# An eleventh pattern buffer, a ring of 23, and another order of the work in an attention and feed-forward kernel

## The chip, the cores and the metric

The kernel runs on one core of a Trainium2 chip. The metric is the device time of one execution in microseconds (us). Three timed runs of the kernel before took 674.03 to 674.70 us, with the median at 674.62. The core has five engines: PE (TensorE, matmuls into the eight banks of PSUM), ACT (ScalarE), DVE (VectorE), POOL (GpSimd) and SP (SyncE, which issues the DMAs here). Each works through its own list of instructions in order, and waits on semaphores for the others.

## The reference

The input x has 2048 rows of 640. It is normalised by rows, and three things are added up: x itself, an attention and a feed-forward part that both read the normalised rows.

```python
xn = _layernorm(x, axis=-1)
# attention: 32 heads of 20, one k and one v for all heads
q = (xn @ wq) as [32 heads, 2048, 20];  k = xn @ wk;  v = xn @ wv
p = softmax(q @ k.T * 20 ** -0.5)
A = (p @ v) put together as [2048, 640] @ wo
# feed-forward, 1536 wide, squared ReLU
h = relu(xn @ w1 + b1);  B = (h * h) @ w2 + b2
return x + A + B
```

The softmax's 32 x 2048 x 2048 exponentials are the bulk of the work.

## The kernel before

**Tiles.** Queries come in 4 chunks (`qc`) of 512 rows, heads in 8 groups (`g`) of 4: 32 blocks (`b`). A block has 16 tiles of 128 keys. A tile of a block is four scores matmuls (one per head, side by side on four row groups of PE, L1395), each filling one bank with 128 keys x 512 queries. One bank of such scores is called a head-tile here: there are 32 x 16 x 4 = 2048.

**Two ways to an exponential.** Most tiles go through ACT: one ACTIVATE (L1676, in `S_EXP`) reads two or three neighbouring banks and writes exp into slots of a ring `PT` with `RING` slots of 512 columns. A slot is free again when the PV matmul (L1981, in `PVblk`) has read it. The other tiles go through DVE: it turns a bank of scores into 16-bit integers that are the bits of a bf16 power of two (L1775, in `S_P1`), into a pattern buffer of `pbx`; there are `NPB` buffers of four heads. Three further buffers of the tile get the same pattern plus a constant (phases), by DVE (L1796, in `S_PH`) or by POOL as 64-bit integer additions (L1858, in `S_PHP`). All four patterns are multiplied with v, the three phases with weighted copies `vp`, so that their sum smooths the staircase of the first. `ph_take` (L1751) hands out free pattern buffers.

**PV and norm.** PV matmuls of a block add up in one bank; v has a column of ones, so that the softmax's denominators come along. When a block is done, `norm` (L2005) copies the bank (`Tn`, L2026), sends the denominators through DMAs (`dn`, reciprocal L2031, `kT`'s spare rows, `Rb` spread over the partitions), multiplies (L2042) into `OTs`, and `pack` moves the rows by DMA into `OTp`, where the head rows of a chunk stand closely for the output matmuls. The last three blocks (`norm_last`, L2049) do this with transposes on DVE instead. The last two blocks' rows go to a buffer of their own, `OT7`, and meet rows of `wo` in `wo_u`.

**The other work.** The feed-forward matmuls (L1013), the projections of q, k and v, and the output matmuls are put in between as units with due positions (`U`, `S_MISC`). PE is kept from going idle by filler matmuls (L1896, `S_FILL`).

**What sets the order.** The whole order is worked out while the program is built. `Sched` (L262) runs the streams (`S_QK`, `S_EXP`, `S_P1`, ...) against a model of the engines' durations and writes one list of instructions per engine. Its choices (how many banks to an exponential, how many DVE head-tiles beside them, how early scores are issued before ACT is free, when a unit is due) come from `PLAN` (L95): one row of 35 parameters for each half of a block, 64 rows. `pick` (L1371) draws some of the choices from a hash of a row's `seed`, for one choice in `nz`. So a changed constant moves every instruction after it.

**Memory shared over time.** At the opening, x lies in the first five pattern buffers (`PBX`); `S_PBF` hands them over when all rows are normalised. `stats6` holds the rows' statistics at the opening (L741, `stats`). `b2r` holds the bias b2 on all partitions from about block 4 on (`weights`, L679).

Of the kernel before, what the change touches and what calls it, by code (L numbers as in the profile page):

```python
# [6 lines left out]
BF16 = mybir.dt.bfloat16  # L7
F32 = mybir.dt.float32
# [9 lines left out]
G = H // HPG  # L18
# [34 lines left out]
RING = 24  # L53
NPB = 10
# [134 lines left out]
RG = ([4, 6], [6, 8], [8, 12], [12, 16])  # L189
XG, TG = '', 'X11'  # L190
TEDP = -1
X0W = 0
KEP = 0.85
TRW = False
TELAND = 4500.0
RSP = -1
TEP = 0.95
G2 = "S7"
NLAST = 3
NTN = 3  # L200
DAX = 2000.0
DAL, DBL, DCL, NBL, QSL, XRL = 4200.0, 2900.0, 7600.0, 2300.0, 2700.0, 3600.0
CLTL = 9000.0
PVEND = 0.5
PTOL = 500.0
PXAT = (31.2, 31.4, 31.6, 31.8)
LATEP = 0.9
PVU = 0.8
LATE = 0.2
DSOLO = (0, 3, 400.0, 300.0)  # L210
DHUNG = 2
DMAXR = 2

# [309 lines left out]
def bass_parallel_sum__grouped_kv_mqa__dense_activation_squared_relu__prompt_kernel(nc, A_x, A_wq, A_wk, A_wv, A_wo, B_x, B_w1, B_b1, B_w2, B_b2, out):  # L523
    es = ExitStack()
    with es:
# [46 lines left out]
        T2 = qpk  # L572
        OTs = sb("OTs", [128, 2, 512], BF16)
        OTp = sb("OTp", [128, 2, NOT, 512], BF16)
        OT7 = sb("OT7", [128, 2, 512], BF16)
        wo_p = sb("wo_p", [128, NOT, D], BF16)
        wo_u = sb("wo_u", [128, 2, D], BF16)
        b2r = sb("b2r", [128, D], BF16)
# [1698 lines left out]
```

## Time and profile before

| | |
|---|---|
| timed runs | 674.62, 674.70, 674.03 us |
| the profiled execution | 674.94 us, of which the span from the first to the last instruction is 673.2 |
| exponentials on ACT | 642 (510 of two banks, 132 of three), 648.9 us busy |
| patterns from scores, DVE | 626 instructions, 412.6 us busy |
| phases on DVE, on POOL | 99 instructions, 68.2 us; 796 pieces, 452.0 us |
| scores matmuls | 2048, 251.1 us busy |
| PV matmuls on PT, with vp, on the pattern itself | 1416, 1896, 632 |

How to read it: the page gives busy times of each engine, and groups of instructions by line with their tile names (written <- read), their count, busy time, mean duration of one, the engine's idle time just before them and what ended it. Matmuls are pipelined, so a busy PE need not be PE at its limit; what tells is who waited for whom. "128x1024" from `ps` is an exponential of two banks, "128x1536" one of three. The weights' loads of a matmul are listed as PEld, and a wait of a group of matmuls shows there.

### The profile page before, as it was taken

What the parts mean: (1) busy time and instruction counts of PE and PEld (TensorE: products, weight loads), DVE (VectorE), ACT (ScalarE), POOL (GpSimd) and SP (SyncE); (2) the same over time, 40 slices, a digit from 0 to 9 for tenths busy, and PEclk for the clock granted to TensorE, in tenths of its full rate; (3) what the DMA queues carried; (4) which work ended last, traced back from release to release, by engine and by line L of the source; (5) the groups of instructions that cost most, each with busy time, mean ns of one, the idle gap of its engine ahead of it and who ended that gap; (6) DMA issues with size and microseconds to landing.
All of it is one profiled execution on the core that took longest, in us unless ns stands there. A gap on an engine that the chain in (4) does not pass through costs nothing.

```text
span 673.2 us, 23449 instructions
## 1 busy us (share of the span) xinstructions
PE 663.9 (99%) x9838; PEld 224.4 (33%) x9838; DVE 614.3 (91%) x1106; ACT 655.5 (97%) x665; POOL 471.7 (70%) x837
## 2 busy tenths in 40 slices
PE   8999999999999999999999999999999999999998
PEld 5332222222223333332222333332323333333334
DVE  7979999999999798989999879899999898998897
ACT  6999999999999999999999999999999999999993
POOL 3547777777786776878777786877788777676700
PEclk9999999999999999999999999999999999999999
DMA  9541222311111121110111121210111012121001
GB/s 259 131 71 48 58 57 72 85 46 35 24 20 35 33 46 43 26 42 17 26 29 29 26 61 22 48 35 19 31 31 23 20 42 49 38 48 26 13 2 42
DMA packets 39915, 30.43 MB, mean 45 GB/s; under 512 B 22818, under 2 KB 34819, under 8 KB 39811
## 3 DMA queue, kind: packets, MB, share of 16 engines
q1 hardware_dynamic: 39810, 28.93, 18.3%
q8 instruction: 79, 1.29, 0.8%
q14 instruction: 26, 0.20, 0.1%
HBM read 11.49 MB, written 2.62 MB: 21 GB/s over the span
## 4 chain that ended last, share of the span: by engine, by line
PE 83%; ACT 8%; DVE 7%; DMA 1%; issue 0%; SPq 0%
PE ps L1981 32%; PE ps L1395 26%; PE ps L1013 24%; ACT PT L1676 8%; DVE pbx L1775 3%; DVE stats L741 1%; DMA OTp<-OTs 0%; DMA pbx<-in_A_x_dram 0%; DVE pbx L1796 0%; DVE vp L1065 0%; DVE hT_tmp L1149 0%; SPq L2092 0%; DVE xnT L956 0%; DVE mv L744 0%; DVE qpk L1104 0%
## 5 line engine op out<-in xcount | busy, mean ns | idle before, releaser
L1676 ACT ACTIVATE PT<-ps 128x1024 bf16<-128x1024 f32 (+1 forms) x642 | 648.9, 1176 | 3.0 <-PE ps L1395 2.6
L1858 POOL INT64_ADD pbx<-pbx x796 | 452.0, 585 | 149.3 <-DVE pbx L1796 75.7
L1775 DVE TENSOR_SCALAR pbx<-ps 128x512 int16<-128x512 f32 (+1 forms) x626 | 412.6, 688 | 44.9 <-PE ps L1395 41.5
L1395 PE MATMUL ps<-qT,kT 20*128 20x512 bf16 x2048 | 251.1, 384 | 1.2 <-DVE hT_tmp L1149 0.5
L1981 PE MATMUL ps<-pbx,vp 128*32 128x512 bf16 x1896 | 174.7, 383 | 0.1
L1395 PEld LDWEIGHTS ps<-qT,kT 20*128 20x128 bf16 x2048 | 63.2, 91 | 241.3 <-ACT PT L1676 164.0
L1981 PE MATMUL ps<-PT,vx 128*32 128x512 bf16 x1416 | 134.8, 384 | 1.0 <-ACT PT L1676 0.8
L1013 PE MATMUL ps<-xnT,w_sb 128*32 128x512 bf16 x960 | 73.6, 383 | 0.2
L1013 PE MATMUL ps<-w_sb,big 128*32 128x320 bf16 x1536 | 72.4, 301 | 0.0
L1796 DVE TENSOR_SCALAR pbx<-pbx 128x2048 int16<-128x2048 int16 x99 | 68.2, 697 | 0.3
L1981 PEld LDWEIGHTS ps<-pbx,vp 128*32 128x32 bf16 x1896 | 46.3, 95 | 48.9 <-issue 31.7
L1981 PE MATMUL ps<-pbx,vx 128*32 128x512 bf16 x632 | 61.7, 384 | 0.4 <-DVE pbx L1775 0.4
L1981 PEld LDWEIGHTS ps<-PT,vx 128*32 128x32 bf16 x1416 | 35.2, 95 | 45.4 <-issue 33.1
L1013 PEld LDWEIGHTS ps<-w_sb,big 128*32 128x32 bf16 x1536 | 34.1, 96 | 25.9 <-issue 18.4
L1149 DVE TENSOR_SCALAR hT_tmp<-ps,b1col 128x512 bf16<-128x512 f32 x48 | 35.6, 742 | 0.8 <-PE ps L1013 0.5
L1013 PE MATMUL ps<-wo_p,OTp 128*32 128x320 bf16 (+1 forms) x608 | 31.8, 302 | 0.4 <-DMA OTp<-OTs 0.3
L1013 PE MATMUL ps<-xnT,wq_sb 128*32 128x512 bf16 x375 | 29.0, 383 | 0.0
L1013 PEld LDWEIGHTS ps<-xnT,w_sb 128*32 128x32 bf16 x960 | 19.0, 95 | 28.7 <-issue 17.7
L792 POOL TENSOR_SCALAR big<-pbx,rstd,nmr 128x640 bf16<-128x640 bf16 x16 | 14.8, 934 | 18.8 <-DVE mv L744 11.0
L1981 PEld LDWEIGHTS ps<-pbx,vx 128*32 128x32 bf16 x632 | 16.4, 95 | 21.0 <-issue 11.3
L2026 DVE COPY Tn<-ps 128x512 f32<-128x512 f32 x29 | 19.8, 683 | 0.3 <-PE ps L1981 0.2
L2042 DVE TENSOR_TENSOR OTs<-Tn,Rb 128x512 bf16<-128x512 f32 x29 | 20.1, 693 | 0.0
(93 smaller groups left out, 190.1 us busy)
## 6 DMA issues: line engine op xcount, KB each, us to landing
Rb<-kT SPq DMA_DIRECT2D x29, 256.0 KB
xres<-in_A_x_dram SPq DMA_DIRECT2D x16, 160.0 KB
out_dram<-out_sb SPq DMA_DIRECT2D x16, 160.0 KB
qT<-qpk SPq DMA_DIRECT2D x105, 20.0 KB
OTp<-OTs SPq DMA_DIRECT2D x105, 20.0 KB
pbx<-in_A_x_dram SPq DMA_DIRECT2D x3, 640.0 KB
w_sb<-in_B_w_dram SPq DMA_DIRECT2D x1, 1920.0 KB
w_sb<-in_B_w_dram SPq DMA_DIRECT2D x12, 160.0 KB, 2.3
```

Of the source, the lines that this page charges most:

```text
L741: v = yield (lambda hh=hh: Req(("dve", 400.0, 470.0, [lambda e: e.bn_stats(out=stats6[:, st, hh, :], in_=x_sb[:, st, 320 * hh:320 * hh + 3 ...
L792: alts = [("dve", 400.0, 440.0, [lambda e: e.tensor_scalar(out=xn(st), in0=x_sb[:, st, :], scalar1=rstd[:, st:st + 1], scalar2=nmr[:, st:s ...
L1013: return lambda e: e.matmul(ps[32 * j:32 * j + m, b_[0], 0:n], Lj, R, start=first, stop=last, tile_position=(0, 32 * j))
L1149: v = yield Req(("dve", 658.0, 742.0, [lambda e: e.tensor_scalar(out=hT_tmp[:, k, :], in0=ps[:, b_[0], :], scalar1=b1col[:, f:f + 1], scal ...
L1395: ins.append(lambda e, i=i, b=b, t=t, h=h: e.matmul(ps[:, i, :], kT[32 * h:32 * h + DH, t * 128:(t + 1) * 128], qT[32 * h:32 * h + DH, b % ...
L1676: op = yield Req(("act", d_, d_ + 107.0, [lambda e, slot=slot, n=n, src=src: e.activation(out=PT[:, slot:slot + n, :], in_=ps[:, src, :], ...
L1775: return Req(("dve", d_, d_ + 82.0, [lambda e: e.tensor_scalar(out=PB[:, k, hsl, :], in0=ps[:, bk:bk + np_, :], scalar1=OFFS, scalar2=0.0, ...
L1796: return Req(("dve", 600.0, 684.0, [lambda e: e.tensor_scalar(out=PB[:, k, :, :], in0=PB[:, s, :, :], scalar1=PH_D[j], scalar2=None, op0=A ...
L1858: return lambda e: e.int64_add(PB8[:, k, c0 // 4:c1 // 4], PB8[:, s, c0 // 4:c1 // 4], int(PH_D[j]) * 0x0001000100010001)
L1981: ins = [(lambda e, h=h, first=first, last=last: e.matmul(ps[32 * h:32 * h + 32, bk, :], lhs, rhs[h], start=first, stop=last, tile_positio ...
L2026: v = yield Req(("dve", 600.0, 682.0, [lambda e: e.tensor_copy(out=Tn[:, tb, :], in_=ps[:, pvb, :])]), (lambda: None if oldt() is None els ...
L2042: w = yield Req(("dve", NM_D, NM_D + 82.0, [lambda e: e.tensor_tensor(out=dst[:, :], in0=Tn[:, tb, :], in1=Rb[:, a, :], op=ALU.mult)]), (l ...
```

## The change

1. `NPB` goes from 10 to 11: one more pattern buffer of 4096 bytes on each partition. `RING` goes from 24 to 23 slots of 1024 bytes.
2. The last two blocks' rows no longer have a buffer of their own (`OT7`, 2048 bytes). They go to column tile `NOT - 1` (the fifth) of `OTp`: block 30 to the half of `OTp` that chunk 3 uses, whose fifth tile chunk 3 leaves empty; block 31 to the other half, which chunk 2 used. So block 31's last step also waits for chunk 2's output matmuls.
3. The opening's statistics `stats6` (768 bytes) lie in `b2r`, and the load of `b2r` names all 16 row tiles' normalisations.
4. The due times that the build assumes for the denominators' transfer: `DAL` from 4200 to 3800 ns, and `DAX`, added for the first seven blocks, from 2000 to 2500.
5. All 64 rows of `PLAN` are new: 61 have another seed, 54 another `nz`, and in some rows other parameters differ (`DPH` in 11, `mq` in 10, `mshift` and `W32` in 9, `broken` in 8, others in fewer).

```diff
-RING = 24
-NPB = 10
+RING = 23
+NPB = 11
...
-DAX = 2000.0
-DAL, DBL, DCL, NBL, QSL, XRL = 4200.0, 2900.0, 7600.0, 2300.0, 2700.0, 3600.0
+DAX = 2500.0
+DAL, DBL, DCL, NBL, QSL, XRL = 3800.0, 2900.0, 7600.0, 2300.0, 2700.0, 3600.0
...
-        stats6 = sb("stats6", [128, ST, 2, 6], F32)
+        b2r = sb("b2r", [128, D], BF16)
+        stats6 = b2r[:, 0:ST * 24].bitcast(F32).rearrange("p (st h k) -> p st h k", st=ST, h=2)
...
-        OT7 = sb("OT7", [128, 2, 512], BF16)
...
-        b2r = sb("b2r", [128, D], BF16)
...
-            dma("sp", "b2r", ..., [done[f"X{ST - 1}"]], 3500.0, size=160.0)
+            dma("sp", "b2r", ..., get(*[f"X{st}" for st in range(ST)]), 3500.0, size=160.0)
...
-                    return (lambda j: OT7[:, t - NOT + 1, stl * 128 + 32 * j:stl * 128 + 32 * j + 32]), wo_u[:, t - NOT + 1, cs]
+                    return (lambda j: OTp[:, NOT - t, NOT - 1, stl * 128 + 32 * j:stl * 128 + 32 * j + 32]), wo_u[:, t - NOT + 1, cs]
...
+                if b == NBLK - 1:
+                    o = get(*[f"O{QC - 2}_{st}_{hh}" for st in range(4 * QC - 8, 4 * QC - 4) for hh in range(2)])
+                    if o is None:
+                        return None
+                    dd = dd + o
...
-            dst = OT7[:, g - G + 2, :] if qc == QC - 1 and g >= G - 2 else OTs[:, a, :]
+            dst = OTp[:, G - 1 - g, NOT - 1, :] if qc == QC - 1 and g >= G - 2 else OTs[:, a, :]
```

The first row of `PLAN`, before and after:

```diff
-    (640, 3500.0, 600.0, 6000.0, 0, 900.0, 12, 2, 0.0, 3, 60.0, 600, 4.0, 2000.0, 2, 0.3, 0, 0.0, 0.0, 4, 0.5, 2, (0, 3, 400.0, 300.0), 1, 247198604, 3, 1.0, 2.0, 4, 99, 2000.0, -1, 400.0, 600.0, 560),
+    (640, 3500.0, 600.0, 6000.0, 0, 900.0, 12, 2, 0.0, 3, 60.0, 600, 4.0, 2000.0, 2, 0.3, 0, 0.0, 0.0, 4, 0.5, 2, (0, 3, 400.0, 300.0), 1, 885727164, 12, 1.0, 2.0, 4, 99, 2000.0, -1, 400.0, 600.0, 560),
```

More of the change, by code (lines that the diff above doesn't have):

```diff
@@ L686, in weights @@
                 dma("sp", f"w2_{k}", lambda e, k=k: e.dma_start(w2_sb[:, k, :], w2v[:, k, :]), [done[f"X{ST - 1}"]], 3500.0, size=160.0, after=done[f"w2_{k - 1}"].done if k else 0.0)
-            dma("sp", "b2r", lambda e: e.dma_start(b2r[:], B_b2.rearrange("(o n) -> o n", o=1).to_broadcast([128, D])), [done[f"X{ST - 1}"]], 3500.0, size=160.0)
+            dma("sp", "b2r", lambda e: e.dma_start(b2r[:], B_b2.rearrange("(o n) -> o n", o=1).to_broadcast([128, D])), get(*[f"X{st}" for st in range(ST)]), 3500.0, size=160.0)
             yield Until(lambda: have(*[f"w2_{k}" for k in range(FT)]))
@@ L2053, in norm_last @@
             w_ = 512 // nh
-            dst = OT7[:, g - G + 2, :] if qc == QC - 1 and g >= G - 2 else OTs[:, a, :]
+            dst = OTp[:, G - 1 - g, NOT - 1, :] if qc == QC - 1 and g >= G - 2 else OTs[:, a, :]
             own = qc == QC - 1 and g >= G - 2
```

118 rows, old and new, of the table PLAN are left out of this document.

## The prediction

> **What bounds the kernel now.** I read the page first (busy times, then the waits), then the groups of ScalarE kept apart by shape, then the windows, then the opening and the tail instruction by instruction. The page and the waits:
>
> ```profile
> span 673.2 us, 23449 instructions
> PE 663.9 (99%) x9838; PEld 224.4 (33%) x9838; DVE 614.3 (91%) x1106; ACT 655.5 (97%) x665; POOL 471.7 (70%) x837
> ```
> ```profile
> PEld ps L1395 <- ACT PT L1676: 164.0, 429, 0.9
> ...
> PEld ps L1395 <- DVE pbx L1775: 48.7, 130, 0.4
> ...
> DVE pbx L1775 <- PE ps L1395: 41.5, 99, 1.3
> ...
> ACT PT L1676 <- PE ps L1395: 2.6, 7, 0.9
> ```
>
> PE looks busiest at 99%, but its score matmuls (L1395) stood still 164.0 us in all for ScalarE to empty a bank. ScalarE waited for PE 2.6 us in all. So the exponentials (L1676) set the pace and PE follows. The windows say the same for the whole stretch of exponentials, from the first at 10.9 us to the last, which ends at 663.0:
>
> ```profile
> 10.89 3.29 ACT L1676 ACTIVATE PT<-ps 128x1024 bf16<-128x1024 f32 x3 [0.89 <-PE ps L1395]
> ```
> ```profile
> 645.21 17.80 ACT L1676 ACTIVATE PT<-ps 128x1024 bf16<-128x1024 f32 x16
> ```
> ```profile
> 43.00:663.10 620.10, 617.34 (x9149) 200.49 (x9150) 571.07 (x972) 619.00 (x613) 452.20 (x797) 1.00 0.15 36
> ```
>
> In that last row the fourth busy time, 619.00 of 620.10, is ScalarE's, and the clock granted to TensorE is 1.00. The time is therefore: opening (10.9) + exponentials end to end (652.1) + tail (10.2). The profiled execution took 674.94 us, 1.7 above its span; the three timed runs have their median at 674.62. I work out a difference and put it on the median.
>
> What one exponential costs on ScalarE is its pitch, not its recorded duration (records overlap by the write-back). Two stretches without waits give it:
>
> ```profile
> L1676 ACT ACTIVATE PT<-ps 128x1024 bf16<-128x1024 f32 x29 | 26.8, 1073 | 0.0
> ```
> ```profile
> L1676 ACT ACTIVATE PT<-ps 128x1536 bf16<-128x1536 f32 x7 | 10.4, 1530 | 0.0
> ```
>
> The first (window 179.1 to 205.7): 29 of two banks in 26.8 us, less some 0.15 of the last one's write-back, is **0.918** each. The second is from the window 645.3 to 663, where the 16 of the row at 645.21 are 9 of two banks and 7 of three: (17.80 - 0.15 - 9 x 0.918) / 7 = **1.34** for three banks.
>
> **The change part by part.** The lists of instructions of the two built kernels can be counted; where each wait falls cannot.
>
> *Exponentials.* Before: 510 of two banks and 132 of three, 1416 head-tiles of scores. After: 502 and 136, 1412. One tile of four heads goes to the other path (VectorE writes the exponential's bits, four patterns), 159 tiles instead of 158. ScalarE: 8 x 0.918 removed, 4 x 1.34 added: 7.34 - 5.36 = **-1.97 us**, all of it on the path that sets the pace. ScalarE's other instructions are the same.
>
> [...]
>
> *VectorE and GpSimd.* Evictions of scores into patterns (L1775): 632 bank-loads become 636. Additions of a constant on patterns by VectorE (L1796): 99 become 103; GpSimd's share falls from 375 to 374 patterns. Pitches:
>
> ```profile
> 107.89 2.40 DVE pbx L1775 x4
> ```
> ```profile
> 661.62 1.90 DVE L1796 TENSOR_SCALAR pbx<-pbx 128x2048 int16<-128x2048 int16 x3
> ```
> ```profile
> 106.00:148.00 42.00, 41.89 (x550) 11.90 (x546) 42.00 (x75) 41.92 (x44) 32.45 (x55) 1.00 0.27 69
> ...
> 295.00:400.00 105.00, 104.17 (x1528) 33.64 (x1525) 94.72 (x161) 104.87 (x103) 83.18 (x150) 1.00 0.13 29
> 400.00:505.00 105.00, 105.00 (x1557) 33.40 (x1549) 95.89 (x165) 104.95 (x103) 80.37 (x142) 1.00 0.15 34
> ```
>
> 4 x 0.60 + 4 x 0.63 = 4.9 us more on VectorE. I cost it at nothing because of where it falls. VectorE (third busy time) is full from 106 to 148, but only 90 to 91% busy from 295 to 505, some 20 us free. In the lists the evictions up to the copy that ends block 8 are 178 before and 177 after, so the additional ones come later, where the slack is. Were that cover gone, it would cost up to 4.9 us.
>
> *PE.* Twelve matmuls more on patterns with vp, four more with vx, four fewer on PT, and the twelve filler matmuls (L1896) gone: 9840 in both lists. PE waits 164 us for ScalarE, so this costs nothing.
>
> *The memory.* OT7 becomes parts of OTp that no one else uses at that time; the last block's multiplication now also waits for block row 2's output matmuls, long done. The statistics lie in b2r, whose load now names all 16 normalisations instead of the last; it stands behind the loads of w2 either way. Nothing. Ring of 23: an exponential would have to wait for the matmul that reads its slot (L1981). Among what ended ScalarE's idle time only L1395 appears, so 24 slots never bound. Bounds 0 and +2 us (a slot is worth 0.46 us of ScalarE's time, at a handful of places); I take 0, the nearer to the row.
>
> *SP's queue.* The lists hold the same transfers, in another order around the denominators' round trip (dn, kT, Rb).
>
> ```profile
> L2042 DVE TENSOR_TENSOR OTs<-Tn,Rb 128x512 bf16<-128x512 f32 x29 | 20.1, 693 | 0.0
> ...
> L2031 DVE RECIPROCAL rd<-dn 128x16 f32<-128x16 f32 x29 | 7.0, 242 | 0.0
> ```
> ```profile
> w_sb<-in_B_w_dram SPq DMA_DIRECT2D x12, 160.0 KB, 2.3
> ```
>
> Its readers on VectorE never idled. The due time of dn, 0.4 us earlier after block 6, is still 3.8 us, and twenty times the bytes land in 2.3. Nothing.
>
> *Opening.* The order of VectorE's and PE's instructions up to 45 us is different. Before:
>
> ```profile
> 21.67 1.94 ACT L1676 ACTIVATE PT<-ps 128x1024 bf16<-128x1024 f32 x2
> ...
> 22.89 0.74 DVE L1037 TENSOR_SCALAR kT<-ps,nk 128x512 bf16<-128x512 f32 x1
> ...
> 23.68 0.62 PE L1981 MATMUL ps<-PT,vx 128*32 128x512 bf16 x8 [0.21 <-DVE kT L1037]
> ...
> 23.78 0.21 ACT L750 ACTIVATE vtmp<-mv 128x4 f32<-128x4 f32 x1 [0.17 <-DVE mv L744]
> ...
> 24.23 0.39 PE L1395 MATMUL ps<-qT,kT 20*128 20x512 bf16 x4
> ...
> 24.56 1.26 PE L1013 MATMUL ps<-xnT,w_sb 128*32 128x512 bf16 x20
> ...
> 24.68 1.02 ACT L1676 ACTIVATE PT<-ps 128x1024 bf16<-128x1024 f32 x1 [0.45 <-PE ps L1395]
> ...
> 26.20 1.02 ACT L1676 ACTIVATE PT<-ps 128x1024 bf16<-128x1024 f32 x1 [0.49 <-PE ps L1395]
> ```
>
> The scores at 24.23 stood behind PV matmuls that waited for VectorE's copy of kT, the next ones behind twenty matmuls of the hidden layer. ScalarE lost 0.45 and 0.49. After, three score matmuls stand ahead of those PV matmuls, and the hidden layer comes in pieces of four and eight. Against that: kT's copy now follows two more half-row statistics and two small ones (about 0.95 us), and ScalarE's vtmp stands one exponential earlier, so that it waits for the mv of row tile 11 instead. Going down the list with the durations above: 24 head-tiles end at 23.61 - 0.92 = 22.7. The mv that vtmp needs comes without kT's copy ahead of it, some 0.66 earlier than now, at 23.1. Then vtmp (0.24), an exponential, rstd (0.2) and three exponentials follow: the 32nd head-tile ends at 27.2 to 27.3. Before it ended at 26.20 + 2 x 0.92 = 28.0. I take **-0.7**. Bounds: -2.0 (all idle time before exponentials up to 43 us gone) and +0.9 (the later kT comes through in full).
>
> *Tail.* Before, from the end of the last score matmuls on, PE is never idle:
>
> ```profile
> 661.33 2.49 PE ps L1981 x44
> 663.82 0.27 PE ps L1013 x8
> 664.09 0.22 PE ps L1981 x4
> 664.31 5.76 PE ps L1013 x168
> ```
>
> 48 of 512 columns and 176 of 320, which is 0.226 and 0.137 per four. After, the list has 24 and 212 there: 6 x 0.226 + 53 x 0.137 = 8.62 instead of 8.74. But the last exponential is of two banks instead of three, so that 1.34 - 0.92 = 0.42 less of PE's tail lies beside ScalarE: **+0.30**. The chain of the last block on VectorE still has 18 groups of matmuls (2.5 us) beside it, as before.
>
> *Waits in between.* From 43 to 663 us, 485 exponentials of two banks and 128 of three:
>
> ```profile
> L1676 ACT ACTIVATE PT<-ps 128x1024 bf16<-128x1024 f32 x485 | 467.9, 1092 | 0.9 <-PE ps L1395 0.6
> L1676 ACT ACTIVATE PT<-ps 128x1536 bf16<-128x1536 f32 x128 | 193.2, 1512 | 0.1
> ```
>
> At their pitches they need 485 x 0.918 + 128 x 1.34 = 616.7 of 620.1 us, so 3.4 us are lost in small waits (most of them inside the records). Every order from 30 us on is new. I take the same 3.4, with bounds -1.7 and +3.4 (half, and twice, as many such waits).
>
> **Sum:** -1.97 - 0.7 + 0.30 = -2.37, or 672.3 us on the median of 674.62.
>
> **Rivals.** A measurement of this kernel can tell about 0.2% (1.35 us) from no change.
>
> 1. *The saved ScalarE time turns into waits.* The next after ScalarE is PE: scores that come a little late, as at 24.23. For it: every one of 638 batches has a new neighbour. Against it: only 3.4 us are lost now in 620. It needs 1.5 to 3 us more of small waits, and gives 674.6. The ring of 23 (+2 us) ends here as well. Chance 0.26.
> 2. *VectorE becomes the bound (slower).* In 106 to 148 us VectorE has nothing left (42.00 of 42.00). A late eviction there keeps a bank, the next scores wait, and ScalarE with them. The place is after the copy that ends block 1, where the list has 24 evictions until the next copy instead of 20. If the 4.9 us of additional work, whatever its place, find no slack, the time is 672.3 + 4.9 = 677.2. It decides from 3.7 us (2.37 + 1.35) of that work uncovered. Against it: the count up to block 8 is one lower. Chance 0.09.
> 3. *PE's clock falls (slower).* The fillers, 12 matmuls or 3 groups in the whole kernel, are gone. If half the clock were granted over the tail's 5.76 us, it would be 678. The rows have 1.00 throughout, and the longest of PE's 429 waits for ScalarE is 0.9 us. Chance 0.01. [...]
> 4. *The change does not do what it says.* The eleventh buffer moves one tile of 512; with no new order, -1.97 alone is left, 672.7, still faster. It lies in the forecast's own range.
>
> **How the numbers follow.** Forecast (672.3, its own range 670.0 to 673.2): 0.64. Rival 1: 0.26. Rivals 2 and 3: 0.10. Faster by over 0.2% is below 673.27, slower is above 675.97. The range: at the low end -2.37 with half of the opening's remaining 1.3 us and the small waits' 1.7 gone is 669.9; at the high end it goes through rival 1 (674.6) and 0.7 us of rival 2, to 675.3. It leaves out most of rivals 2 and 3 and about 0.08 at the low end.
>
> **What would show it.** ScalarE: 638 exponentials, busy time about 2 us lower, idle before them no more than 3 us. If the idle or the recorded durations' excess grows by 2 us, rival 1 holds. Opening: the 32nd head-tile ends near 27.3 and no wait of 0.45 at 24 to 27 us. Tail: PE ends about 8.4 us after the last exponential starts. Rival 2 would show as a VectorE at 100% in more windows than 106 to 148 and L1775 as what ends ScalarE's or PE's waits. The prediction is wrong if the exponentials, first start to last end, take more than 651 us.

## The result, and the profile after

The kernel after takes 675.72 us (median of 19 runs, 675.11 to 678.68), the kernel before 674.52 in the same comparison (19 runs). The ratio is 1.0023, 95% interval 1.0016 to 1.0030: slower by 1.2 us, where the prediction had 2.3 us less. The profiled execution took 675.21 us, of which the span is 673.5.

The page of the kernel after, its span and busy times:

```profile
span 673.5 us, 23451 instructions
...
PE 663.1 (98%) x9838; PEld 223.5 (33%) x9838; DVE 616.7 (92%) x1120; ACT 652.9 (97%) x661; POOL 468.6 (70%) x827
```

ScalarE is busy 2.6 us less than before and still the span is 0.3 us longer. So somewhere it stood still for longer. Its groups by shape (busy time, mean ns, then the idle time before them), and below them those of the kernel before:

```profile
L1675 ACT ACTIVATE PT<-ps 128x1024 bf16<-128x1024 f32 x502 | 483.4, 1077 | 1.7 <-PE ps L1394 1.4
L1675 ACT ACTIVATE PT<-ps 128x1536 bf16<-128x1536 f32 x136 | 202.9, 1497 | 4.6 <-PE ps L1394 4.5
```

```profile
L1676 ACT ACTIVATE PT<-ps 128x1024 bf16<-128x1024 f32 x510 | 491.7, 1089 | 2.9 <-PE ps L1395 2.6
L1676 ACT ACTIVATE PT<-ps 128x1536 bf16<-128x1536 f32 x132 | 198.8, 1510 | 0.1
```

The counts are as predicted, 502 and 136. The idle time is 6.3 us instead of 3.0, and the list of waits says that one wait of 3.1 us made up about half of it (total, times, longest):

```profile
PEld ps L1394 <- DVE pbx L1774: 57.3, 142, 3.6
...
ACT PT L1675 <- PE ps L1394: 5.8, 5, 3.1
...
DVE xres L1171 <- DMA xres<-in_A_x_dram: 3.6, 1, 3.6
...
PE ps L1394 <- DVE pbx L1774: 3.1, 1, 3.1
```

Three engines, PE twice over (weight loads and matmuls), have a longest wait of 3 to 4 us. Whether it is one event is read from the timeline. SP's queue there (start, duration of the issue):

```profile
287.63 3.58 SPq L2096 DMA_DIRECT2D OTp<-OTs  x5
291.31 0.62 SPq L2041 DMA_DIRECT2D Rb<-kT  x1
291.98 0.48 SPq L1225 DMA_DIRECT2D out_dram<-out_sb  x1
292.50 1.68 SPq L1168 DMA_DIRECT2D xres<-in_A_x_dram  x1
```

The last row loads 128 rows of x once more (160 KB, row block 7) for the residual. The chain of work through this stretch shows how long it took, and who went on behind it:

```profile
292.50 8.15 DMA xres<-in_A_x_dram
300.65 0.02 issue
300.68 0.49 DVE xres L1171
301.17 0.61 DVE pbx L1774
301.78 0.05 issue
301.83 0.40 PE ps L1394 x4
```

VectorE, TensorE and ScalarE in the timeline, with the idle time and its releaser in brackets:

```profile
300.68 0.49 DVE L1171 TENSOR_TENSOR xres<-xres,b2r 128x640 bf16<-128x640 bf16 x1 [3.58 <-DMA xres<-in_A_x_dram]
```
```profile
301.83 0.40 PE L1394 MATMUL ps<-qT,kT 20*128 20x512 bf16 x4 [3.14 <-DVE pbx L1774]
```
```profile
302.27 2.37 ACT L1675 ACTIVATE PT<-ps 128x1536 bf16<-128x1536 f32 x2 [3.05 <-PE ps L1394]
306.04 4.20 ACT L1675 ACTIVATE PT<-ps 128x1536 bf16<-128x1536 f32 x4 [1.40 <-PE ps L1394]
```

One load lands 8.15 us after its issue. VectorE works in order, so its bias addition (L1171) holds up the evictions of scores behind it for 3.58 us; the banks stay full, PE has no place for scores for 3.14 us, and ScalarE has nothing to read for 3.05 us. A second wait of 1.40 us follows at 306. The windows show what PE's clock did meanwhile (PE's busy time is the second number, the granted clock the third from the end):

```profile
298.00:300.00 2.00, 0.69 (x16) 0.11 (x4) 0.00 (x0) 1.22 (x2) 0.00 (x0) 1.00 0.18 52
300.00:302.00 2.00, 0.17 (x4) 0.10 (x4) 1.32 (x3) 0.00 (x0) 0.73 (x2) 1.00 0.01 3
302.00:303.00 1.00, 0.98 (x11) 0.24 (x7) 1.00 (x2) 0.73 (x1) 0.70 (x2) 0.72 0.00 0
303.00:304.00 1.00, 1.00 (x15) 0.35 (x16) 1.00 (x3) 1.00 (x2) 0.66 (x2) 0.50 0.00 0
304.00:305.00 1.00, 1.00 (x16) 0.26 (x8) 0.82 (x2) 0.64 (x1) 0.62 (x2) 0.50 0.09 21
305.00:306.00 1.00, 1.00 (x16) 0.20 (x12) 0.50 (x1) 0.00 (x0) 1.00 (x2) 0.57 0.09 21
306.00:308.00 2.00, 2.00 (x30) 0.56 (x30) 1.67 (x4) 1.96 (x2) 1.83 (x3) 1.00 0.09 21
```

After its idle time PE gets half its clock for some 3.4 us. It is fully busy then, and yet ScalarE catches up with it and waits again.

To see what the rest of the kernel did, I took from the records, for each exponential, the time from the end of the one before it to its own end, less its pitch (0.917 us for two banks, 1.343 for three), and added these up by stretch of the span:

```
                   first starts  0-30   30-60  294-312  rest   last ends  span
before             10.89         2.60   1.28   0.16     3.02   663.01     673.22
after              10.84         1.48   1.03   4.66     2.73   663.84     673.48
```

Every stretch but one became better, and that one, from 294 to 312 us, took it all back.

### The profile page after: what moved, and what is told of

It reads as the page before. It is cut to its first block, busy times and chain, and to the rows that moved or that the text cites. A ratio compares the mean times of both kernels' runs of the same rounds, so it can differ in the third digit from the quotient of the medians.

```text
span 673.5 us, 23451 instructions
## 1 busy us (share of the span) xinstructions
PE 663.1 (98%) x9838; PEld 223.5 (33%) x9838; DVE 616.7 (92%) x1120; ACT 652.9 (97%) x661; POOL 468.6 (70%) x827
## 4 chain that ended last, share of the span: by engine, by line
PE 70%; ACT 22%; DVE 6%; DMA 2%; issue 0%; SPq 0%
PE ps L1980 27%; PE ps L1394 22%; ACT PT L1675 22%; PE ps L1012 21%; DVE pbx L1774 2%; DVE b2r L740 1%; DMA xres<-in_A_x_dram 1%; DMA pbx<-in_A_x_dram 0%; DVE pbx L1795 0%; DVE mv L743 0%; DVE hT_tmp L1148 0%; DVE xnT L955 0%; DVE Rb L868 0%; PE ps L1049 0%; PE ps L1001 0%
## 5 line engine op out<-in xcount | busy, mean ns | idle before, releaser
L1675 ACT ACTIVATE PT<-ps 128x1024 bf16<-128x1024 f32 x638 | 646.5, 1166 | 6.3 <-PE ps L1394 5.8
L1774 DVE TENSOR_SCALAR pbx<-ps 128x512 int16<-128x512 f32 x636 | 415.1, 682 | 38.6 <-PE ps L1394 35.7
L1795 DVE TENSOR_SCALAR pbx<-pbx 128x2048 int16<-128x2048 int16 x103 | 70.0, 689 | 0.3
```

What stands on the lines that cost most here:

```text
L1675: op = yield Req(("act", d_, d_ + 107.0, [lambda e, slot=slot, n=n, src=src: e.activation(out=PT[:, slot:slot + n, :], in_=ps[:, src, :], ...
L1774: return Req(("dve", d_, d_ + 82.0, [lambda e: e.tensor_scalar(out=PB[:, k, hsl, :], in0=ps[:, bk:bk + np_, :], scalar1=OFFS, scalar2=0.0, ...
L1795: return Req(("dve", 600.0, 684.0, [lambda e: e.tensor_scalar(out=PB[:, k, :, :], in0=PB[:, s, :, :], scalar1=PH_D[j], scalar2=None, op0=A ...
```

## The experiments

**Theory A**: the load stands 1.19 us behind the broadcast `Rb` (256 KB) and comes late for that; VectorE's in-order wait and the clock behind it cost some 4.5 us; the rest of the change gains what the sum says. **Rival B**: PE, at 98%, is the bound, and any time saved turns into another wait. **Rival C**: the load is late for another reason than the broadcast. **Theory on the clock**: the second wait comes from the half clock, not from the backlog.

In most of these, entries of the planned lists were moved after the plan was made, so that nothing else of the order changes; `place(x, y, 0)` puts entry x ahead of y, `place(x, y, 1)` behind it. `xq7` is the load of row block 7, `XB7` its reader L1171, `dc12` the broadcast of block 12. The cuts of code leave out these helpers and other lines at `...`.

### The load ahead of the broadcast

```diff
         sc.run()
...
+        place(find("sp", "xq7"), find("sp", "dc12"), 0)
...
         sc.resolve(...)
```

> The changed kernel, with one entry of SP's list moved: the load of row block 7 (xres, L1168) is issued ahead of the broadcast Rb of block 12 (L2041), not 1.19 us behind it. Theory A (the load stands behind the broadcast's 256 KB, lands 8.15 us after issue, and VectorE's in-order wait for it empties TensorE): the load lands 2.2 to 4 us after issue, L1171 waits for nothing, ScalarE's two waits of 3.05 and 1.40 us at 302 and 306 us go, and the time is 675.7 - 4.5 = 671.2 (670.5 to 672). Rival B (TensorE, at 98%, is the bound, and the saved ScalarE time turns into waits wherever there is room): another wait takes the place, 674 to 675.7. Rival C (the load is late for the five pieces of L2096 issued ahead of it, or for the memory, not for the broadcast): it stays late, lands 6 to 8 us after issue, 674.5 to 675.7.

Measured: **671.49 us** (671.10 to 672.09), ratio to before 0.9954 (0.9943 to 0.9966). The load, now ahead of the broadcast:

```profile
292.17 0.48 SPq L1168 DMA_DIRECT2D xres<-in_A_x_dram  x1
292.75 0.61 SPq L2041 DMA_DIRECT2D Rb<-kT  x1
```

By the trace's semaphore events it landed 2.30 us after its issue, though the same five pieces of L2096 were issued ahead of it. VectorE's wait is gone, and ScalarE's waits in the whole run are down:

```profile
ACT PT L1675 <- PE ps L1394: 2.0, 5, 0.9
```

So one entry of SP's list, moved two places up, is worth 4.2 us against the kernel after, and this version beats both kernels. Rival B falls, and so does the part of rival C that blames the five pieces. A store (L1225) also stood between the broadcast and the load, and the move passed it too; the converse below has none there.

### The reader later, the load as it was

```diff
...
+        later(find("dve", "XB7"), find("dve", "N1_13"), find("dve", "SQ2_0"), find("dve", "SQ2_1"))
```

(`later` moves the reader behind the second entry and lets GpSimd's waits on it go to the neighbours named.)

> The changed kernel, SP's list as it was; in VectorE's list the reader of that load (L1171, the bias added to row block 7) stands seven instructions later, behind the first copy of block 13 (L2030); GpSimd's waits on it go to the neighbouring instructions. Theory A: the load still lands some 8 us after issue, at about 300.6, but VectorE reaches L1171 only at about 301 and waits under 0.3 us; TensorE and ScalarE go on: 671.2 (670.5 to 672), as with the load moved. Rival B: 674 to 675.7, another wait in its place. Rival C says nothing else than A here.

Measured: 672.05 us (671.82 to 672.33), ratio 0.9962 (0.9949 to 0.9975), just above the expected range. The load was as late as before, 8.14 us; its issue and its reader:

```profile
292.60 1.67 SPq L1168 DMA_DIRECT2D xres<-in_A_x_dram  x1
```
```profile
302.27 0.47 DVE L1171 TENSOR_TENSOR xres<-xres,b2r 128x640 bf16<-128x640 bf16 x1
```

No bracket stands behind the reader: nothing was waited for. So here the late load cost next to nothing by itself. What it cost in the kernel after came through the work that stands behind its reader on an engine that works in order.

### Filling PE's idle time

```diff
...
+        fill_ = [(lambda e, h=h: e.matmul(ps[32 * h:32 * h + 32, was["bk"], :], zeros32[:, :], w1_sb[:, 0, 0:512], start=False, stop=False, tile_position=(0, 32 * h))) for h in range(HPG)]
+        place(Op("pe", fill_ * 14, [done["zeros"], done["w1"]], "fill"), gate, 0)
```

(`gate` is the scores entry that waits at 301.8, `was["bk"]` the open PV bank.)

> The changed kernel, with 56 matmuls that add zeros (14 groups of 4, 512 columns, into the open PV bank) put ahead of the scores that wait at 301.8 us; load and reader as they were. Theory A with the clock (TensorE is idle for 3.14 us there, and the granted clock of 0.50 that follows costs the second ScalarE wait, 1.40 us): VectorE's 3.6 us and ScalarE's first wait of about 3.05 us stay, the granted clock from 302 to 306 us is 1.00, the second wait goes, and the time is 675.7 - 1.4 = 674.3 (673.8 to 674.8). Rival D (the second wait is the backlog behind the first, whatever the clock): both waits stay, 675.3 to 676.

Measured: 674.11 us (673.89 to 674.47, 11 runs), 1.6 less than the kernel after; ratio to before 0.9993 (0.9985 to 1.0002). VectorE waited 3.6 us as before, ScalarE's longest wait was 3.1, the second was gone, and the clock stayed up:

```profile
DVE xres L1171 <- DMA xres<-in_A_x_dram: 3.6, 1, 3.6
```
```profile
ACT PT L1675 <- PE ps L1394: 4.5, 4, 3.1
```
```profile
302.00:306.00 4.00, 3.69 (x54) 1.19 (x50) 4.00 (x8) 3.38 (x3) 2.99 (x5) 1.00 0.06 14
```

The clock's part is shown, then: 1.6 of the 4.2 us. It goes with the scatter of the kernel after, too. One stretch of 3.41 us at half clock takes 0.0025 off the mean clock of a span of 673.5 us, so that, as an estimate, mean clocks of 0.997, 0.995 and 0.992 stand for one, two and three such stretches. Of its twelve runs with a mean clock of 0.997, eleven take 675.1 to 675.8 us (one 676.7), the six with 0.995 take 676.1 to 677.0, and the one with 0.992 took 678.68; the 11 filled runs lie within 0.6 us.

### The converse, in the kernel before

```diff
...
+        xb = find("dve", "XB7")
+        later(xb, sc.lists["dve"][xb.idx + 7], find("dve", "SQ2_1"), find("dve", "SQ2_2"))
+        place(find("sp", "xq7"), find("sp", "dc12"), 1)
```

> The converse, in the kernel before: the load of row block 7 is issued directly behind the broadcast Rb of block 12 (0.6 us after it, at about 297.3), and its reader L1172 stands seven instructions later in VectorE's list, where VectorE comes to it at about 301.7. Theory A: the load lands 7.5 to 8.5 us after issue, at about 305, VectorE waits 3 to 4 us, TensorE goes idle behind it, and the kernel before gets slower by 2.5 to 5 us: 677 to 679.5. Rival C (not the broadcast): the load lands within 2.2 to 4 us, by 301.5, and the time is that of the kernel before, 674.5 within 0.5. Rival E (before's order has the slack to take such a wait): the load is late, and the time is 674.5 to 675.5.

Measured: 679.3 us (676.81 to 683.28), ratio 1.0076 (1.0052 to 1.0100). The load landed 6.81 us after its issue, a little earlier than expected, though nothing stood between it and the broadcast. So the store falls as a reason, and rival C with it. VectorE waited 2.38 us, less than the 3 to 4 expected:

```profile
303.89 0.49 DVE L1172 TENSOR_TENSOR xres<-xres,b2r 128x640 bf16<-128x640 bf16 x1 [2.38 <-DMA xres<-in_A_x_dram]
```

The kernel before has the same weak spot; its order just did not touch it. Here too the clock falls behind it (third number from the end), and the runs scatter by 6.5 us. The one with a mean clock of 1.000 took 676.81 us, those with 0.992 took 681.38 and 683.28:

```profile
308.00:310.00 2.00, 2.00 (x18) 0.35 (x14) 1.96 (x4) 1.36 (x2) 1.91 (x4) 0.50 0.06 13
```

### The layout alone, the buffer alone, the search alone

The kernel before with the new memory layout, 10 buffers, a ring of 24 and the old seeds (its lists are those of before, instruction by instruction):

> The kernel before with the new layout alone: b2r over stats6, the last two blocks' rows in OTp (OT7 gone), and the waits that these need; 10 pattern buffers, ring of 24, the old build seeds and landing times, so the instructions of each engine stand in the order of before. Theory A (layout costs nothing; the loss is the one late load): 674.5, within 0.5. Rival F (the shared rows make the last blocks wait for the readers of the old ones): 675 or more, with a longer stretch behind the last exponential.

Measured: 675.0 us, ratio 0.9999 (0.9990 to 1.0009). The layout costs nothing that can be measured here.

```diff
-RING = 24
-NPB = 10
+RING = 23
+NPB = 11
```

> The layout, 11 pattern buffers and the ring of 23, with the old build seeds and landing times: the buffer without the search. The schedule has 650 exponentials, 518 of two banks and 132 of three: 8 two-bank ones more than before. If ScalarE bounds, that is 8 x 0.918 = +7.3 us: 682 (680 to 684). If the eleventh buffer brings something by itself (fewer waits of the eviction for a buffer), the time is under 680.

Measured: 682.21 us (681.26 to 683.14), ratio 1.0111 (1.0097 to 1.0125), as the count of exponentials says.

The new rows of `PLAN`, with `NPB = 10` and `RING = 24`:

> The new build seeds and landing times with 10 pattern buffers and the ring of 24: the search without the buffer. The schedule has 655 exponentials, 528 of two banks and 127 of three: 18 x 0.918 - 5 x 1.34 = +9.8 us against before, if ScalarE bounds and its waits stay: 684.4 (682 to 692, waits of ScalarE on top in a plan that the seeds weren't drawn for).

Measured: 692.89 us (692.67 to 693.10), ratio 1.0269 (1.0255 to 1.0283), 0.9 above the range. The price of the pitches is 9.8 us; ScalarE's small waits beyond 60 us, added up as above, are 12.1 us instead of 3.2, the other 9. Each set of seeds does worse with the other's constants. So these two runs don't take the change apart into a gain of the buffer and a gain of the search.

### The load on another queue

```diff
...
+        sc.lists["sp"].remove(xq)
+        sc.order.remove(xq)
+        xq.eng = "act"
+        place(xq, mark, 1)
```

(`mark` is ScalarE's entry at the same planned time.)

> The changed kernel, with the load of row block 7 issued by ScalarE at the same place in time instead of by SP, behind the same broadcast Rb; all else in its order. If the load is late because it stands behind Rb's packets in SP's own queue, another queue lets it land 2 to 5 us after issue, VectorE's 3.6 us wait goes, and the time is 671.2 to 672.2 (ScalarE pays for the issue, 0.1 to 0.6 us). If it is late because the DMA engines that both queues share are taken by Rb's 256 KB, it lands 6 to 8 us after issue by this queue too, VectorE waits 2 to 3.6 us, and the time is 674 to 676.

Measured: 675.7 us, ratio 1.0019 (1.0010 to 1.0028), no better than the kernel after. The load landed 8.54 us after its issue, where 6 to 8 was expected. The issue and the wait:

```profile
292.47 0.39 ACTq L1168 DMA_DIRECT2D xres<-in_A_x_dram  x1
```
```profile
301.04 0.49 DVE L1171 TENSOR_TENSOR xres<-xres,b2r 128x640 bf16<-128x640 bf16 x1 [3.59 <-DMA xres<-in_A_x_dram]
```

The load's semaphore counts 16 parts. The times at which they came, from the trace's events:

```
kernel after, load issued 292.50:    12 parts by 297.29, the others 299.75 299.76 299.85 300.65
ACT's queue, load issued 292.47:     12 parts by 295.02, the others 300.09 300.10 300.64 301.01
broadcast's own parts, kernel after: 298.86 298.94 298.99 299.38
```

Twelve parts come in time by either queue. Four come only after the broadcast's four. The packets of the load on ACT's queue show the same: 96 of its 128 start by 294.67 us, none between, and the other 32 from 299.33 on, when the broadcast's last packet has ended (299.29). So it is not SP's queue alone that is blocked. The records don't name the DMA engine of a packet. But in the kernel after, four of the broadcast's 128 packets are under way at once in 4.89 of its 6.16 us, and more than four for 3 ns only. With the broadcast's four parts and the load's four late ones of 16 this gives, as an estimate, that the broadcast holds four of the 16 engines, and that a quarter of the load waits for those.

### The broadcast by head

Each head's 32 partitions as a transfer of its own, for block 12 alone (by a condition `b == 12`, left out below) and then for all 29 blocks:

```diff
-lambda e: e.dma_start(Rb[:, a, :], Rr[DH + a:128:32, :].rearrange("h (o n) -> h o n", o=1).to_broadcast([HPG, 32, 512]))
+[lambda e, h=h: e.dma_start(Rb[32 * h:32 * h + 32, a, :], Rr[DH + a + 32 * h:DH + a + 32 * h + 1, :].rearrange("h (o n) -> h o n", o=1).to_broadcast([1, 32, 512])) for h in range(HPG)]
```

> The changed kernel in its own order, with the broadcast Rb of block 12 alone written as four transfers of 64 KB, one for each head (32 partitions each), in place of one of 256 KB over four heads; the load of row block 7 stays behind it. Theory G (the one transfer's 128 packets of 2 KB run on 4 of the 16 DMA engines, 22.9 us of packets in 6 us, and the load's last 4 of 16 parts wait on just those): each of the four spreads over all 16 engines, the last has landed within 3 to 5 us of the first issue, the load, issued some 2 us later than now (four issues of about 0.6 us), lands 2.2 to 3.5 us after its issue, by 297.5, VectorE waits under 0.7 us, and the time is 671 to 672.3. Rival H (the 256 KB take the same time however they are cut, or the single-head transfers run on one engine or few each): the load lands 6 to 9 us after the first broadcast's issue, VectorE waits 2.5 to 5 us, 674.5 to 677.5.

Measured: 677.74 us (676.29 to 678.79), ratio 1.0039 (1.0020 to 1.0059). Theory G falls. It came out worse than rival H too: the load landed 10.75 us after the first broadcast's issue, where H had 6 to 9. Of H's two reasons, the one that a single head's transfer runs on few engines does not hold, by the estimate below. The load now came late on all its parts, and VectorE waited longer:

```profile
302.37 0.49 DVE L1171 TENSOR_TENSOR xres<-xres,b2r 128x640 bf16<-128x640 bf16 x1 [4.99 <-DMA xres<-in_A_x_dram]
```

Two things made it late. SP issued it only at 297.17 instead of 292.50, behind four issues and a store whose own issue took 2.31 us; and it then took 5.18 us to land instead of 2.3. The packet records show the broadcast itself (128 packets of 2 KB in both):

```
kernel after:  292.58 to 298.74 us, mean 179 ns a packet, 22.9 us of packets in all
by head:       292.82 to 300.75 us, mean 653 ns a packet, 83.6 us of packets in all
```

The semaphore shows 64 parts for the four transfers, 16 each, where the one transfer had four and four packets under way at once; so, as an estimate, each did run on 16 engines. But my premise that more engines make it quicker was wrong: each packet takes 3.7 times as long, and the whole takes 7.9 us instead of 6.2, of which up to 1.9 us may be due to the four issues coming one after another. What slows the packets (the reading of one row of `kT` by all engines, or another thing) no run here tells.

> As the run before, with all 29 broadcasts of Rb written by head, in the changed kernel's order. Theory G: no load is late behind any of them; the time is that of the run before, 671 to 672.3, since no other load waited. Against it: SP's queue has 87 issues of some 0.6 us more, which can hold back what stands behind them (the pieces of L2096, the stores): up to +1.

Measured: 681.89 us (680.37 to 685.93), ratio 1.0105 (1.0068 to 1.0142), far above what was expected. Now the multiplication itself waits for the broadcast in some blocks (its profile is of the slowest of the six runs, 685.93 us):

```profile
DVE OTs L2046 <- DMA Rb<-kT: 4.7, 6, 1.5
DVE xres L1171 <- DMA xres<-in_A_x_dram: 4.5, 1, 4.5
```

## Why the prediction was wrong, by its own steps

- **SP's queue, "Nothing": this step failed.** I saw that the lists held the same transfers in another order, and then looked only at the readers of the denominators' round trip (`Rb`, `rd`). Those never idled, after the change either. But `Rb` is also what other transfers stand behind, and the reader that mattered was that of the load `xres`, L1171. For its landing I took the 2.3 us of a 160 KB row without asking what was ahead of that row's transfers. In the trace of before the answer was to be had: the loads issued 3.78 and 5.31 us behind an `Rb` landed 5.45 and 4.17 us after their issue, all those 6.5 us or more behind it within 3.3. The two late ones landed 9.2 and 9.5 us after the broadcast's own issue; for a load 1.19 us behind one this gives, as an estimate, 8.0 to 8.3 us, and 8.15 came. The planner's landing time for this load, `XRL`, 3600 ns, is the same wherever it stands, so a new order could place its reader too early by up to 4.5 us, as measured here. The list of the changed kernel shows the load as the second entry behind `dc12`, and the reader 4.3 us later by the plan.
- **Exponentials, -1.97: right.** 502 and 136, ScalarE's busy time 2.6 us less. With the load moved, first start to last end is 649.7 us (10.90 to 660.61), and 653.0 with the load late: over the 651 that the prediction named as its refutation.
- **Opening, -0.7: right in kind, a little small.** The 32nd head-tile ends at 26.98 us (predicted 27.2 to 27.3; before 28.14, which the prediction had as 28.0). The waits of 0.45 and 0.49 are gone. It isn't steady: in the profile of the run with the load moved it is 27.89, only 0.25 less than before.
- **Tail, +0.30: wrong by 0.9, the other way.** From the last scores to PE's end I had 8.62 us, and it is 8.63 (662.10 to 670.73). But these scores were done 0.62 us before the last exponential could start, against 0.16 before, so PE was 0.46 further on beside it; and the last store ended 2.75 us after PE instead of 3.18. From the end of the last exponential the tail is 9.64 us, 0.57 less than before.
- **Small waits, unchanged: right.** From 30 us on without the one event (columns 30-60 and rest), 3.8 us instead of 4.3.
- **VectorE, PE, memory, ring at nothing: right.** From 106 to 148 us VectorE has 1.5 us to spare where it had none; no exponential waits for a ring slot; the layout alone measures 0.9999.
- **Rival 3, the clock (0.01): its mechanism came, from another cause.** Not the missing fillers, but the late load emptied PE for 3.14 us, and the clock fell to 0.50. The 0.9 us by which the prediction judged it was the longest of PE's waits for ScalarE; this wait was for VectorE's eviction.
- **The sum.** With the load in time the change brings 3.1 us (674.60 to 671.49), or 2.6 with the reader moved instead, against 2.37 in the sum. That these lie near each other is partly luck: in the profile of the run with the load moved, the opening brought 0.25 instead of 0.7, and the tail brought 0.56 where the sum had a loss of 0.30. What was missing is one term: a late load, +4.2 in the median, of which the clock is 1.6.

The slower rival that I named (VectorE as the bound) was not the one that came. The place that I left without a price was a queue whose order changed.

## What to carry to other kernels

Where a change gives a new order, go through the queues too: for each transfer look at what is issued shortly ahead of it, and compare the landing that a planner assumes with the landing behind a large transfer, which the trace before usually holds somewhere. A late transfer cost little where its reader came after the landing (8.14 us to land, 672.05 us in all), and 4.2 us where an engine that works in order waited for it; so ask how long the engines behind go idle, since here 3.14 us of TensorE's idle time were paid for a second time in its clock (1.6 us). And before giving up a searched order that came out slower, look for a single long wait in it: moving one entry by hand turned 0.23% slower into 0.46% faster.

## What the runs showed of the hardware

- **The broadcast over four heads held 4 of the 16 DMA engines for some 6 us** (packets from 292.58 to 298.74), as an estimate from the four packets under way at once and the parts of the semaphores, and a load issued behind it had 12 of 16 parts in time and 4 late, by SP's queue and ACT's alike (above). The load's issue on SP took 1.68 us instead of 0.42 in the kernel after, behind the broadcast and a store, but 0.47 in the converse run, directly behind the broadcast; what lengthens it stays open.
- **Cutting it by head made it slower**: 653 ns a packet instead of 179.
- **PE's clock.** An idle time of 3.14 us was followed by a half clock from 302.44 to 305.85 us. From one change of the clock to the next lay whole multiples of 3.413 us (296.96 us of full clock, 87 of them, then one at half; in the trace of before 669.01 us of full clock, 196 of them), and the full clock first began at another time of the span in each of these profiles (5.48 us in the kernel after, 5.42 before, 5.22 with the load on ACT's queue, 6.83 in the converse run). The length of the idle time alone did not decide: 2.60 us in the converse run were followed by a half clock as well, and with all broadcasts by head 1.25 us were, while 1.68 and 1.37 us in that same profile were not. No threshold comes out of these.
- **The kernel before is not free of it.** One of its 17 runs beside the broadcasts by head took 681.45 us at a mean clock of 0.990; there is no trace of that run, and its cause is open.
